# Attention beside a spectral filter on one core: the filter's last product with constants as weights in two parts, and output sums of eleven products for twelve

## The chip, the cores and the metric

The kernel runs on one core of a Trainium2 chip. The metric is the device time of one execution in microseconds, the median of the runs shown. The engines are TensorE (PE, with its weight loads listed as PEld), VectorE (DVE), ScalarE (ACT), GpSimd (POOL) and SyncE (SP); POOL, SP and ACT also issue DMAs, each in its own queue and in program order.

## The reference

Two independent computations of 2048 x 448 results, put side by side:

```python
# A: 16 heads of 28 columns, one shared key and value head
q = (x @ wq).reshape(B, S, H, Dh);  k = x @ wk;  v = x @ wv
p = softmax(einsum("bhqd,bkd->bhqk", q, k) * Dh ** -0.5)
a = einsum("bhqk,bkd->bhqd", p, v).reshape(B, S, H * Dh) @ wo
# B: a filter in the frequency domain
X = rfft2(x, axes=(-2, -1)) * (w_r + 1j * w_i)
b = irfft2(X, (S, D), axes=(-2, -1))
out = concatenate([a, b], axis=-1)
```

## The kernel before

**Precision by parts.** Most large products are made of reduced-precision float32 operands (F32R) in parts: an operand is cast to a high part, and the difference to the original is its low part. A product of two operands is then high x high + low x high + high x low.

**Attention.** The 16 heads stand as four groups g of four heads, each head in 32 rows, of which 28 are used; the four spare rows of the query weights carry columns for keys and values. Queries come in four chunks c of 512. A step is one key block of 128 for one (c, g): four score products (`score`, L1100), one for each head, each into one of seven PSUM banks; four exponentials on ACT (`exps`, L1117) from the bank into a p tile out of a ring of `P_BUFS`; and the value products (`values`, L1132) that read p and add up in bank 7. There are 256 steps. After 16 of them `group_out` (L986) copies bank 7 away, the sums of the exponentials go through DRAM and come back as a broadcast tile R by POOL's queue (L991 to L1000), and `group_norm` (L1008 to L1011) multiplies and splits the result into `oh` and `ol`. R's rows are all 32 of each head. When four groups of a chunk are done, four output units (`w_unit`, for 128 queries each) may run: `wo_mm` (L1020) makes 4 x 3 = 12 products of 448 columns, three for each group, and `wo_out` evicts. The last chunk's output products run at the very end (`partial`, and L1252 for its last group).

**Filter.** The first transform is done ahead of attention. While attention runs, DVE does a radix-2 transform in the tile X, multiplies by the filter and transforms back as background work (`forward`, `inverse`), and stores X to DRAM (`store`, L903). Then for each of eight q: `fft3_load` loads by POOL's queue, two `z_unit`s (L942) make products that DVE copies to SBUF (L948), and two `y_unit`s (L961) multiply by the cosine and sine constants cs3: each has four plain float32 products of 113 columns with z as the weights. DVE combines them (L966 to L975) and SP stores to ob (L977). The tiles of this stage are cut out of X's space (`carve`).

**The order.** It is written out by a plan in the kernel's own Python, which keeps a clock for PE, DVE and ACT with assumed durations, and emits the instructions of each engine in the order in which its loop (the `while done_steps < 256`) reaches them. A cycle of that loop is: scores, then the values of n steps. n is 4 if fill is at hand (over 1.0 us of it by the plan's durations), else 2. Fill are pieces of output units (0.605 each) and z and y units (0.88 each); output and filter units alternate where both are there. A piece is taken where at least six scores of the cycle have been made, two scores lie between pieces, and the cycle's quota (`share`, at least 1.6) isn't used up; the quota may be overrun by the last piece. The values of a cycle are emitted when their last exponential should be done and seven scores (`LEAD`) are ahead of them, or no bank is about to come free. A fill holds one of the seven banks until DVE has evicted it. DVE's work is an event list by the same clock (`after`) and a background list (`todo`).

Of the kernel before, what the change touches and what calls it, by code (L numbers as in the profile page):

```python
# [12 lines left out]
F32 = mybir.dt.float32  # L13
F32R = mybir.dt.float32r
# [3 lines left out]
ALU = mybir.AluOpType  # L18
# [4 lines left out]
S, D, H = 2048, 448, 16  # L23
DH = D // H
DF = D // 2 + 1
NG = 4
NC = 4
CW = 512
NK = 4
SCALE = DH ** -0.5  # L30
BOUND = float(np.float32(40.0 / SCALE))
P_BUFS = 20
LEAD = 7
WARM = 8, 8
FIRST = 8
# [60 lines left out]
def kernel(ctx: ExitStack, tc: tile.TileContext, t: dict):  # L96
    nc = tc.nc
    mm = nc.tensor.matmul

    cp = ctx.enter_context(tc.tile_pool(name="cp", bufs=1))  # L100
    dp = ctx.enter_context(tc.tile_pool(name="dp", bufs=1, space=DRAM))
# [6 lines left out]
    vs = cp.tile([128, 16, 32], F32, name="vs")  # L108
    cvec = cp.tile([128, NG, NC], F32, name="cvec")
    bits = cp.tile([1, 1], F32, name="bits")  # L110
    X = cp.tile([128, 2, 32, 113], F32, name="X")
    t1 = dp.tile([64, 2, 2, 32 * 113], F32, name="t1")
    t2 = dp.tile([128, 2, 32 * 113], F32, name="t2")

# [11 lines left out]
    fc, xb, ff = {}, {}, {}  # L126
# [86 lines left out]
    with tc.tile_pool(name="f1", bufs=2) as f1[0], tc.tile_pool(name="w1", bufs=1) as w1, ExitStack() as ctx1:  # L213
# [145 lines left out]

        def load_const(name, shape):  # L360
            def go():
                cons[name] = cp.tile(shape, F32, name=name)
                nc.sync.dma_start(cons[name], t[name])
            return add(SP, 0.4, go, loads[1, 1], kb=32)

# [294 lines left out]

    ap = ctx.enter_context(tc.tile_pool(name="ap", bufs=2))
    pp = ctx.enter_context(tc.tile_pool(name="pp", bufs=P_BUFS))
    V = nc.vector
    TT, STT = V.tensor_tensor, V.scalar_tensor_tensor

# [6 lines left out]
    def after(when, dur, f, *a):  # L672
        heapq.heappush(events, (when, next(serial), dur, f, a))
# [14 lines left out]
    def wide(n):  # L688
        return 0.165 + 0.00107 * n

    woh = ap.tile([128, NG, D], F32R, name="woh", bufs=1)
    wol = ap.tile([128, NG, D], F32R, name="wol", bufs=1)
    fc["cs3"] = ap.tile([113, 4, 113], F32, name="cs3", bufs=1)
    nc.gpsimd.dma_start(fc["cs3"], t["cs3"])

    late, held, early = {}, [None], deque()

# [62 lines left out]

    def wo_split(g):
        V.tensor_copy(woh[:, g], wo[g])
        TT(wol[:, g], wo[g], woh[:, g].bitcast(F32), op=ALU.subtract)


    t1v = t1.rearrange("(r k) l u (n f) -> r (k l u) n f", r=2, f=113)
# [139 lines left out]
                after(clk["dve"] + 3.0, 0.0, fft3_load, k)  # L906


    Xf = X.rearrange("p r n f -> p (r n f)")
    taken = [0]  # L910

    def carve(p, n):
        o = taken[0]
        taken[0] += n
        return Xf[:p, o:o + n]

    c2t = [carve(128, 904).rearrange("p (u j f) -> p u j f", u=2, f=113) for _ in range(2)]
    fit = [carve(128, 512).rearrange("p (j f) -> p j f", f=128) for _ in range(2)]
    zt = [[carve(113, 512).rearrange("p (r j n) -> p r j n", r=2, n=64) for _ in range(2)] for _ in range(2)]
    mt = [carve(128, 226).rearrange("p (k f) -> p k f", f=113) for _ in range(2)]  # L920
    y1t = [carve(128, 452).rearrange("p (k h f) -> p k h f", k=2, f=113) for _ in range(2)]
    yot = [carve(128, 452).rearrange("p (k f) -> p k f", f=113) for _ in range(2)]

    work = {"z": deque(), "w": deque()}
    cur, last_kind = [None], ["w"]
# [3 lines left out]
    def fft3_load(q):  # L929
        if q > 7:  # L930
            return
        nc.gpsimd.dma_start(c2t[q % 2].rearrange("p u j f -> p u (j f)"), t2[:, :, 452 * q:452 * q + 452])
        nc.gpsimd.dma_start(fit[q % 2], t["fi"][:, 4 * q:4 * q + 4])
        after(clk["dve"] + (10.0 if q < 2 else 6.0), 0.0, work["z"].extend, [z_unit(q, 0), z_unit(q, 1)])

    def z_unit(q, e):
        w = (113, 112)[e]

        def go(b):
            pz = view(bank[b], 4, 128)  # L940
            for j in range(4):
                mm(pz[:w, j], c2t[q % 2][:, e, j, :w], fit[q % 2][:, j], start=True, stop=True)  # L942
            if e == 1:
                after(clk["pe"] + 1.2, 0.0, fft3_load, q + 2)
            after(clk["pe"] + 1.2, 0.72, out, b)

        def out(b):
            V.tensor_copy(zt[q % 2][e][:w], view(bank[b], 4, 128)[:w].rearrange("p j (r n) -> p r j n", r=2))  # L948
            free[b] = clk["dve"] + 0.1
            if e == 1:  # L950
                after(clk["dve"] + 0.2, 0.0, work["z"].extendleft, [y_unit(q, 1), y_unit(q, 0)])
        return [(0.88, go)]

    def y_unit(q, v):
        js = slice(2 * v, 2 * v + 2)

        def go(b):
            py = view(bank[b], 4, 113)
            ze, zo = zt[q % 2]
            for k, (z, w, r) in enumerate(((ze, 113, 0), (zo, 112, 0), (zo, 112, 1), (ze, 113, 1))):  # L960
                mm(py[:, k], z[:w, r, js], fc["cs3"][:w, k], start=True, stop=True)  # L961
            after(clk["pe"] + 1.2, 1.2, out, b)

        def out(b):
            py, m, y1 = view(bank[b], 4, 113), mt[v], y1t[v]
            V.tensor_copy(m, py[:, 2:4])  # L966
            TT(y1[:, :, 0], py[:, 0:2], m, op=ALU.add)
            TT(y1[:, :, 1], py[:, 0:2], m, op=ALU.subtract)
            free[b] = clk["dve"] + 0.1
            after(clk["dve"], 0.8, last)  # L970

        def last():
            y1, yo = y1t[v], yot[v]
            TT(yo[:, 0:2], y1[:, 0], y1[:, 1], op=ALU.add)
            TT(yo[:, 2:4], y1[:, 0], y1[:, 1], op=ALU.subtract)  # L975
            r0 = (2 * q + v) * 128
            nc.sync.dma_start(t["ob"][r0:r0 + 128], yo)  # L977
        return [(0.88, go)]


    oh, ol, osb = {}, {}, {}
    normed, taken_out = [0] * NC, [0]

    def group_out(c, g):
# [10 lines left out]
    def group_sums(c, g, rs, rd):  # L995
        V.reciprocal(rs, rs)
        nc.gpsimd.dma_start(rd.rearrange("i (a b) -> (i a) b", b=16), rs)
        R = ap.tile([128, CW], F32, name="R", bufs=1)
        for i in range(4):
            nc.gpsimd.dma_start(R[32 * i:32 * i + 32], rd[i:i + 1].to_broadcast([32, CW]))  # L1000
        after(clk["dve"] + 12.0, 2.1, group_norm, c, g, R)

    def group_norm(c, g, R):
        if g == 0:
            oh[c] = ap.tile([128, NG, CW], F32R, name="oh")
            ol[c] = ap.tile([128, NG, CW], F32R, name="ol")
        o = osb[c, g]
        TT(o, o, R, op=ALU.mult)  # L1008
        h = oh[c][:, g]
        V.tensor_copy(h, o)  # L1010
        TT(ol[c][:, g], o, h.bitcast(F32), op=ALU.subtract)  # L1011
        normed[c] += 1
        if normed[c] == NG and c < NC - 1:
            after(clk["dve"] + 0.3, 0.0, work["w"].extend, [w_unit(c, k) for k in range(4)])

    def wo_mm(p, c, k, gs):
        s = slice(k * 128, k * 128 + 128)
        for g in gs:
            for n, (x, w) in enumerate(((oh, woh), (ol, woh), (oh, wol))):
                mm(p, x[c][:, g, s], w[:, g], start=(g == 0 and n == 0), stop=(g == NG - 1 and n == 2))  # L1020

    def wo_out(p, c, k):
        y = ap.tile([128, D], F32, name="ya")
# [17 lines left out]
    def w_unit(c, k):  # L1041
        def go(g):
            def f(b):
                wo_mm(bank[b][:, :D], c, k, (g,))
                if g == NG - 1:
                    after(clk["pe"] + 0.9, 0.65, out, b)
            return f

        def out(b):
            wo_out(bank[b][:, :D], c, k)  # L1050
            free[b] = clk["dve"] + 0.1
        return [(0.605, go(g)) for g in range(NG)]


    def switch(mode):
# [96 lines left out]
        for i in range(8):  # L1152
            after(18.0 + 2.0 * i, 0.0, spread, i)
    w0 = 5.0 if FIRST == 8 else 28.0
    for g in range(NG):
        after(w0 + 6 * g, 0.0, wo_load, g)
        after(w0 + 6.0 + 6 * g, 1.1, wo_split, g)
    for q in range(FIRST, 8):
        after(1.0 + 3.0 * (q - FIRST), 0.0, late_load, q)
        after(6.0 + 9.0 * (q - FIRST), 1.35, late_fold, q, 0)  # L1160
# [18 lines left out]
        b = 4 if rich else 2  # L1179
        return left if left < b + 2 else b  # L1180

    total = 12 * 4 * 0.605 + 32 * 0.88

    def share(n):
        return max(1.6, n * (total - done[0]) / max(250 - done_steps, 3)) if n > 2 else 0.0

    done_steps, quota = 0, 0.0
    n = size()
# [47 lines left out]
    c, g = NC - 1, NG - 1  # L1236
    o = osb[c, g] = qraw[:, g, c * CW:c * CW + CW]
    w3 = ap.tile([128, D], F32, name="w3", tag="ya")
    nc.sync.dma_start(w3, t["wo"][:, g])
# [69 lines left out]
def _layout(A_x, A_wq, A_wk, A_wv, A_wo, B_x, B_w_r, B_w_i):  # L1309
# [13 lines left out]
    z["wo"] = wo.reshape(NG, 128, D).transpose(1, 0, 2)  # L1323
# [18 lines left out]
def _gather(oa, ob):  # L1342
    out = np.empty((1, S, 2 * D), np.float32)
    out[0, :, :D] = oa
    y = ob.reshape(32, 64, 4, 113).transpose(1, 0, 2, 3).reshape(S, 4, 113)
    d = np.arange(113)
    b = out[0, :, D:]
    b[:, d] = y[:, 0]
    b[:, D - d[1:]] = y[:, 1, 1:]
    b[:, D // 2 - d[:112]] = y[:, 2, :112]  # L1350
    b[:, D // 2 + d[1:112]] = y[:, 3, 1:112]
    return out


_OUTS = {"oa": (S, D), "ob": (S, 4, 113)}


# [14 lines left out]
```

## Time and profile before

| | us |
|---|---|
| median of three runs (641.7 to 643.55) | 642.39 |
| the profiled execution | 641.98 |
| its span, first to last instruction | 640.1 |
| PE busy | 633.5 |
| ACT busy | 547.0 |
| DVE busy | 333.3 |

Attention's steps run from about 71 us to 626 us of the span. In the profile a line such as L1132 is a line of the kernel's file; "b L1132 x32" are the instructions that write a bank at that line. The value products show as eight records to a step, so x16 is two steps and x32 four.

### The profile page before, as it was taken

To read this page: it belongs to the slowest core of one execution; us is meant where nothing else is said; L and a number is where in the kernel's file an instruction comes from. 1 tells how busy PE (TensorE), PEld (TensorE's weight loads), DVE (VectorE), ACT (ScalarE), POOL (GpSimd) and SP (SyncE) were. 2 spreads that over 40 slices of the span, in tenths; PEclk is the share of its full clock that TensorE was granted. 3 is DMA by queue.
4 is the path that set the end of the run, shared out by engine and by line. 5 is a ranking of instruction groups with operands and counts; after the bars stand their busy time and mean duration, and the time that the engine had idled before them with its cause. 6 is when DMAs were issued, how large, how long until landed. Compare 5 with 4: busy or idle time off the path is not lost.

```text
span 640.1 us, 11636 instructions
## 1 busy us (share of the span) xinstructions
PE 633.5 (99%) x4380; PEld 358.5 (56%) x4380; DVE 333.3 (52%) x687; ACT 547.0 (85%) x1100; POOL 89.1 (14%) x164
## 2 busy tenths in 40 slices
PE   9999999999999999999999999999999999999997
PEld 7877544444444456554446655655665655564445
DVE  5999615979897977896323222215334310320014
ACT  4644899999999998889999879878888987888991
POOL 1021131101121101010122020020301101020200
PEclk9999999999999999999999999999999999999999
DMA  8766587030334121124444231132415131130002
GB/s 299 255 164 166 134 239 244 18 68 17 97 105 102 42 68 47 32 67 150 151 141 139 64 91 36 49 111 88 115 61 143 32 82 32 50 93 1 19 0 87
DMA packets 29667, 62.41 MB, mean 98 GB/s; under 512 B 6798, under 2 KB 18415, under 8 KB 28645
## 3 DMA queue, kind: packets, MB, share of 16 engines
q1 hardware_dynamic: 21850, 40.36, 23.1%
q0 software_dynamic: 7328, 20.72, 10.8%
q8 instruction: 35, 0.57, 0.4%
q10 hardware_dynamic: 432, 0.57, 0.3%
q14 instruction: 22, 0.18, 0.1%
HBM read 29.63 MB, written 15.02 MB: 70 GB/s over the span
## 4 chain that ended last, share of the span: by engine, by line
PE 88%; ACT 0%; issue 0%; DVE 0%; ACTq 0%
PE b L1100 41%; PE b L1132 36%; PE b L1020 6%; PE b L961 2%; PE b L942 2%; PE b L1252 0%; PE b L163 0%; ACT yb L1035 0%; DVE yb L1038 0%; ACTq L1036 0%
## 5 line engine op out<-in xcount | busy, mean ns | idle before, releaser
L1117 ACT ACTIVATE p<-b 128x512 f32<-128x512 f32 x1024 | 506.7, 768 | 46.4 <-PE b L1100 45.4
L1100 PE MATMUL b<-qa,ka 128*128 128x512 f32 x1024 | 284.7, 411 | 0.5 <-PEq L617 0.5
L1100 PEld LDWEIGHTS b<-qa,ka 128*128 128x128 f32 x1024 | 182.1, 188 | 128.2 <-ACT p L1117 83.9
L1132 PE MATMUL b<-p,vs 128*32 128x512 f32 x2048 | 240.0, 597 | 0.0
L1132 PEld LDWEIGHTS b<-p,vs 128*32 128x32 f32 x2048 | 56.5, 109 | 120.9 <-issue 119.3
L986 DVE COPY qraw<-b 128x512 f32<-128x512 f32 x15 | 10.4, 692 | 82.0 <-PE b L1132 82.0
L1024 DVE COPY ya<-b 128x448 f32<-128x448 f32 x12 | 7.5, 624 | 65.1 <-PE b L1020 64.0
L991 POOL DMA_DIRECT2D sd<-qraw x15 | 8.8, 587 | 218.8 <-DVE qraw L986 218.8
L827 DVE SCALAR_TENSOR_TENSOR X<-w,X 128x226 f32<-128x226 f32 (+2 forms) x72 | 34.1, 473 | 2.4
L1000 POOL DMA_DIRECT2D R<-rd x60 | 30.2, 508 | 34.9 <-DMA rd<-rs 34.9
L966 DVE COPY X<-b 128x226 f32<-128x226 f32 x16 | 6.2, 390 | 45.3 <-ACT p L1117 43.9
L321 ACT ACTIVATE qraw<-b 128x512 f32<-128x512 f32 x16 | 9.4, 599 | 19.5 <-PE b L317 19.4
L948 DVE COPY X<-b 113x512 f32<-113x512 f32 (+1 forms) x16 | 11.1, 691 | 28.6 <-ACT p L1117 22.7
L317 PE MATMUL b<-xh,wqh 128*128 128x512 f32 x64 | 24.6, 416 | 0.4 <-DVE xh L265 0.4
L1008 DVE TENSOR_TENSOR qraw<-qraw,R 128x512 f32<-128x512 f32 x15 | 10.3, 685 | 26.7 <-DMA R<-rd 26.7
L317 PE MATMUL b<-xh,wql 128*128 128x512 f32 x64 | 23.0, 390 | 0.0
L1020 PE MATMUL b<-woh,oh 128*128 128x448 f32 x60 | 22.1, 369 | 0.0
L1020 PE MATMUL b<-wol,oh 128*128 128x448 f32 x60 | 22.0, 366 | 0.0
L1020 PE MATMUL b<-woh,ol 128*128 128x448 f32 x60 | 21.9, 366 | 0.0
L820 DVE SCALAR_TENSOR_TENSOR w<-X 128x113 f32<-128x113 f32 (+2 forms) x56 | 17.7, 353 | 0.1
L961 PEld LDWEIGHTS b<-cs,X 113*128 113x128 f32 (+1 forms) x128 | 16.8, 191 | 1.4
L317 PE MATMUL b<-xl,wqh 128*128 128x512 f32 x48 | 17.3, 391 | 0.0
(113 smaller groups left out, 511.4 us busy)
## 6 DMA issues: line engine op xcount, KB each, us to landing
qa<-qa SPq DMA_DIRECT2D x15, 512.0 KB
X<-t POOLq DMA_DIRECT2D x16, 452.0 KB, 5.4
xb<-xb SPq DMA_DIRECT2D x8, 512.0 KB
qa<-qh SPq DMA_DIRECT2D x60, 64.0 KB
qa<-ql SPq DMA_DIRECT2D x60, 64.0 KB
R<-rd POOLq DMA_DIRECT2D x60, 64.0 KB, 2.2
t<-bs SPq DMA_DIRECT2D x16, 226.0 KB
wf<-w POOLq DMA_DIRECT2D x8, 452.0 KB, 4.2
```

Of the source, the lines that this page charges most:

```text
L317: mm(pq[c, g], w[:, j, gs], x[:, j], start=(j == 0 and n == 0), stop=(j == 3 and n == 1))
L820: STT(out, y, sy, x, op0=ALU.mult, op1=ALU.add if c > 0 else ALU.subtract)
L827: todo(226 * n, lambda d=d, q=q: STT(both(d), t[0].rearrange("p r n f -> p r (n f)"), q, both(a), op0=ALU.mult, op1=ALU.add))
L942: mm(pz[:w, j], c2t[q % 2][:, e, j, :w], fit[q % 2][:, j], start=True, stop=True)
L948: V.tensor_copy(zt[q % 2][e][:w], view(bank[b], 4, 128)[:w].rearrange("p j (r n) -> p r j n", r=2))
L961: mm(py[:, k], z[:w, r, js], fc["cs3"][:w, k], start=True, stop=True)
L986: V.tensor_copy(o, bank[7])
L1000: nc.gpsimd.dma_start(R[32 * i:32 * i + 32], rd[i:i + 1].to_broadcast([32, CW]))
L1020: mm(p, x[c][:, g, s], w[:, g], start=(g == 0 and n == 0), stop=(g == NG - 1 and n == 2))
L1100: mm(bank[b], ka[:, kc * 128:(kc + 1) * 128], qa[c, g][:, h], start=True, stop=True)
L1117: nc.scalar.activation(p, bank[b], AF.Exp, scale=SCALE)
L1132: mm(bank[7][32 * i:32 * i + 32], vs[:, kc], pt.pop(4 * st + i), start=(kc == 0), stop=(kc == 15))
```

## The change

In the filter's last product the constants become the weights, in a high and a low part (`csh`, `csl`), and z the moving operand, also split into two parts by DVE at its eviction. A y unit is then two sums of three F32R products of 256 columns in place of four plain float32 products of 113. The result stands transposed, and ob's layout changes with it; DVE's last two operations are done once for a pair of units.

In the output product of the first three chunks, the low part of group 0's result is stored to DRAM (`lows`) and loaded from there into the spare rows of `oh` (four groups) and of `ol` (groups 1 to 3). The output weights carry group 0's rows in their spare rows, in seven variants. So the product of group 0's low part needs no instruction of its own: 11 products for 12. R is filled in 28 of 32 rows only, its spare rows are set to zero once. The output units become available 7.0 us after the last norm by the plan's clock (0.3 before).

For the space of this, `P_BUFS` goes from 20 to 17, X moves to a pool of its own that is closed when the last filter stage opens (`fft3_open`), and some constants move to a pool of the start. cs3's load moves from the start of attention to `fft3_open`. The plan's durations and the quota's least value change.

```diff
-P_BUFS = 20
+P_BUFS = 17
...
-    X = cp.tile([128, 2, 32, 113], F32, name="X")
...
     pp = ctx.enter_context(tc.tile_pool(name="pp", bufs=P_BUFS))
+    xp = ctx.enter_context(ExitStack())
+    X = xp.enter_context(tc.tile_pool(name="xp", bufs=1)).tile([128, 2, 32, 113], F32, name="X")
...
-    woh = ap.tile([128, NG, D], F32R, name="woh", bufs=1)
+    woh = ap.tile([128, 7, D], F32R, name="woh", bufs=1)
     wol = ap.tile([128, NG, D], F32R, name="wol", bufs=1)
-    fc["cs3"] = ap.tile([113, 4, 113], F32, name="cs3", bufs=1)
-    nc.gpsimd.dma_start(fc["cs3"], t["cs3"])
+    csh = ap.tile([113, 4, 113], F32R, name="csh", bufs=1)
+    csl = ap.tile([113, 4, 113], F32R, name="csl", bufs=1)
...
     def wo_split(g):
         V.tensor_copy(woh[:, g], wo[g])
-        TT(wol[:, g], wo[g], woh[:, g].bitcast(F32), op=ALU.subtract)
+        if g < NG:
+            TT(wol[:, g], wo[g], woh[:, g].bitcast(F32), op=ALU.subtract)
...
+    def fft3_open():
+        xp.close()
+        p3 = xp.enter_context(tc.tile_pool(name="p3", bufs=2))
+        for q in range(2):
+            fb["c2", q] = p3.tile([128, 2, 4, 113], F32, name="c2")
+            fb["fi", q] = p3.tile([128, 4, 128], F32, name="fi")
+            for e in range(2):
+                fb["z", q, e] = [p3.tile([113, 2, 4, 64], F32R, name=f"z{n}{e}") for n in "hl"]
+        cs = scratch()[:113, :452].rearrange("p (k f) -> p k f", k=4)
+        nc.gpsimd.dma_start(cs, t["cs3"])
+        todo(452, lambda: V.tensor_copy(csh, cs))
+        todo(452, lambda: TT(csl, cs, csh.bitcast(F32), op=ALU.subtract))
...
     def z_unit(q, e):
...
-            after(clk["pe"] + 1.2, 0.72, out, b)
+            after(clk["pe"] + 1.2, 1.4, out, b)
 
         def out(b):
-            V.tensor_copy(zt[q % 2][e][:w], view(bank[b], 4, 128)[:w].rearrange("p j (r n) -> p r j n", r=2))
+            pz = view(bank[b], 4, 128)[:w].rearrange("p j (r n) -> p r j n", r=2)
+            h, l = (x[:w] for x in fb["z", q % 2, e])
+            V.tensor_copy(h, pz)
+            TT(l, pz, h.bitcast(F32), op=ALU.subtract)
...
     def y_unit(q, v):
-        js = slice(2 * v, 2 * v + 2)
 
         def go(b):
-            py = view(bank[b], 4, 113)
-            ze, zo = zt[q % 2]
-            for k, (z, w, r) in enumerate(((ze, 113, 0), (zo, 112, 0), (zo, 112, 1), (ze, 113, 1))):
-                mm(py[:, k], z[:w, r, js], fc["cs3"][:w, k], start=True, stop=True)
-            after(clk["pe"] + 1.2, 1.2, out, b)
+            py = view(bank[b], 2, 256)
+            for k in range(2):
+                kind, e, r = ((0, 0, 0), (2, 1, 1), (1, 1, 0), (3, 0, 1))[2 * v + k]
+                w = (113, 112)[e]
+                zh, zl = (x[:w, r].rearrange("p j n -> p (j n)") for x in fb["z", q % 2, e])
+                for n, (c, z) in enumerate(((csh, zh), (csh, zl), (csl, zh))):
+                    mm(py[:113, k], c[:w, kind], z, start=(n == 0), stop=(n == 2))
+            after(clk["pe"] + 1.2, 2.65 if v else 1.25, out, b)
 
         def out(b):
...
+            y = y1[v] = scratch()[:113, :768].rearrange("p (s n) -> p s n", s=3)
+            V.tensor_copy(y[:, 2], py[:, 1])
+            TT(y[:, 0], py[:, 0], y[:, 2], op=ALU.add)
+            TT(y[:, 1], py[:, 0], y[:, 2], op=ALU.subtract)
+            free[b] = clk["dve"] + (-1.3 if v else 0.1)
+            if v:
+                a, c = y1.pop(0), y1.pop(1)
+                for h, op in enumerate((ALU.add, ALU.subtract)):
+                    last(h, op, a, c)
+
+        def last(h, op, a, c):
+            yo = fp.tile([113, 2, 256], F32, name="yo", tag="bs")
+            TT(yo, a[:, :2], c[:, :2], op=op)
+            nc.sync.dma_start(t["ob"][:, q, h], yo)
+        return [(0.73, go)]
...
+    R = ap.tile([128, CW], F32, name="R", bufs=1)
+    V.memset(R, 0.0)
...
         for i in range(4):
-            nc.gpsimd.dma_start(R[32 * i:32 * i + 32], rd[i:i + 1].to_broadcast([32, CW]))
+            nc.gpsimd.dma_start(R[32 * i:32 * i + DH], rd[i:i + 1].to_broadcast([DH, CW]))
...
-        if normed[c] == NG and c < NC - 1:
-            after(clk["dve"] + 0.3, 0.0, work["w"].extend, [w_unit(c, k) for k in range(4)])
+        if c < NC - 1:
+            if g == 0:
+                lows[c] = dp.tile([128, CW], F32, name="lows", bufs=2)
+                nc.sync.dma_start(lows[c], ol[c][:, 0].bitcast(F32))
+            rows = lows[c].rearrange("(i m r) n -> r i m n", i=4, r=4)
+            if g == NG - 1:
+                for r in range(4):
+                    nc.sync.dma_start(oh[c][DH + r::32].bitcast(F32), rows[r, :, :4])
+                    nc.sync.dma_start(ol[c][DH + r::32, 1:].bitcast(F32), rows[r, :, 4:7])
+                after(clk["dve"] + 7.0, 0.0, work["w"].extend, [w_unit(c, k) for k in range(4)])
...
-            for n, (x, w) in enumerate(((oh, woh), (ol, woh), (oh, wol))):
-                mm(p, x[c][:, g, s], w[:, g], start=(g == 0 and n == 0), stop=(g == NG - 1 and n == 2))
+            spare = c < NC - 1
+            for n, (x, w, m) in enumerate(((oh, woh, g), (oh, wol, g), (ol, woh, g + 3 * spare))):
+                if n < 2 or g or not spare:
+                    mm(p, x[c][:, g, s], w[:, m], start=(g == 0 and n == 0), stop=(g == NG - 1 and n == 2))
...
-        return [(0.605, go(g)) for g in range(NG)]
+        return [(0.605 if g else 0.403, go(g)) for g in range(NG)]
...
-    for g in range(NG):
-        after(w0 + 6 * g, 0.0, wo_load, g)
-        after(w0 + 6.0 + 6 * g, 1.1, wo_split, g)
+    for g in range(7):
+        at = w0 + 6 * g if g < NG else 60.0 + 6 * g
+        after(at, 0.0, wo_load, g)
+        after(at + 6.0, 1.1, wo_split, g)
...
-    total = 12 * 4 * 0.605 + 32 * 0.88
+    total = 12 * 2.22 + 16 * (0.88 + 0.73)
 
     def share(n):
-        return max(1.6, n * (total - done[0]) / max(250 - done_steps, 3)) if n > 2 else 0.0
+        return max(1.8, n * (total - done[0]) / max(250 - done_steps, 3)) if n > 2 else 0.0
...
+    wo = wo.reshape(NG, 4, 32, D)[[0, 1, 2, 3, 1, 2, 3, 3]]
+    wo[:7, :, DH:] = wo[0, :, :DH].reshape(4, 7, 4, D).transpose(1, 0, 2, 3)
+    z["wo"] = wo.reshape(8, 128, D).transpose(1, 0, 2)
...
-_OUTS = {"oa": (S, D), "ob": (S, 4, 113)}
+_OUTS = {"oa": (S, D), "ob": (113, 8, 2, 2, 256)}
```

More of the change, by code (lines that the diff above doesn't have):

```diff
@@ L361, in go @@
             def go():
-                cons[name] = cp.tile(shape, F32, name=name)
+                cons[name] = (cp if name in ("mask", "ident") else w1).tile(shape, F32, name=name)
                 nc.sync.dma_start(cons[name], t[name])
@@ L906, in store @@
                 after(clk["dve"] + 3.0, 0.0, fft3_load, k)
[L909 to L922, printed above, removed]
+    fb = {}
+    def fft3_open():
[10 more added lines that the diff above has]
+        todo(452, lambda: TT(csl, cs, csh.bitcast(F32), op=ALU.subtract))
     work = {"z": deque(), "w": deque()}
@@ L931, in fft3_load @@
             return
-        nc.gpsimd.dma_start(c2t[q % 2].rearrange("p u j f -> p u (j f)"), t2[:, :, 452 * q:452 * q + 452])
-        nc.gpsimd.dma_start(fit[q % 2], t["fi"][:, 4 * q:4 * q + 4])
+        if not fb:
+            fft3_open()
+        nc.gpsimd.dma_start(fb["c2", q % 2].rearrange("p u j f -> p u (j f)"), t2[:, :, 452 * q:452 * q + 452])
+        nc.gpsimd.dma_start(fb["fi", q % 2], t["fi"][:, 4 * q:4 * q + 4])
         after(clk["dve"] + (10.0 if q < 2 else 6.0), 0.0, work["z"].extend, [z_unit(q, 0), z_unit(q, 1)])
@@ L941, in go @@
             for j in range(4):
-                mm(pz[:w, j], c2t[q % 2][:, e, j, :w], fit[q % 2][:, j], start=True, stop=True)
+                mm(pz[:w, j], fb["c2", q % 2][:, e, j, :w], fb["fi", q % 2][:, j], start=True, stop=True)
             if e == 1:
                 after(clk["pe"] + 1.2, 0.0, fft3_load, q + 2)
-            after(clk["pe"] + 1.2, 0.72, out, b)
+            after(clk["pe"] + 1.2, 1.4, out, b)
         def out(b):
-            V.tensor_copy(zt[q % 2][e][:w], view(bank[b], 4, 128)[:w].rearrange("p j (r n) -> p r j n", r=2))
+            pz = view(bank[b], 4, 128)[:w].rearrange("p j (r n) -> p r j n", r=2)
+            h, l = (x[:w] for x in fb["z", q % 2, e])
+            V.tensor_copy(h, pz)
+            TT(l, pz, h.bitcast(F32), op=ALU.subtract)
             free[b] = clk["dve"] + 0.1
@@ L952, in z_unit @@
         return [(0.88, go)]
+    y1 = {}
     def y_unit(q, v):
-        js = slice(2 * v, 2 * v + 2)
         def go(b):
-            py = view(bank[b], 4, 113)
-            ze, zo = zt[q % 2]
-            for k, (z, w, r) in enumerate(((ze, 113, 0), (zo, 112, 0), (zo, 112, 1), (ze, 113, 1))):
-                mm(py[:, k], z[:w, r, js], fc["cs3"][:w, k], start=True, stop=True)
-            after(clk["pe"] + 1.2, 1.2, out, b)
-        def out(b):
[L965 to L981, printed above, removed]
+            py = view(bank[b], 2, 256)
[5 more added lines that the diff above has]
+                    mm(py[:113, k], c[:w, kind], z, start=(n == 0), stop=(n == 2))
@@ new lines, in go @@
+            after(clk["pe"] + 1.2, 2.65 if v else 1.25, out, b)
+        def out(b):
+            py = view(bank[b], 2, 256)[:113]
+            y = y1[v] = scratch()[:113, :768].rearrange("p (s n) -> p s n", s=3)
[7 more added lines that the diff above has]
+                    last(h, op, a, c)
@@ L982 @@
+        def last(h, op, a, c):
[3 more added lines that the diff above has]
+        return [(0.73, go)]
+    oh, ol, osb, lows = {}, {}, {}, {}
+    R = ap.tile([128, CW], F32, name="R", bufs=1)
+    V.memset(R, 0.0)
     normed, taken_out = [0] * NC, [0]
@@ L997, in group_sums, with group_norm @@
         nc.gpsimd.dma_start(rd.rearrange("i (a b) -> (i a) b", b=16), rs)
-        R = ap.tile([128, CW], F32, name="R", bufs=1)
         for i in range(4):
-            nc.gpsimd.dma_start(R[32 * i:32 * i + 32], rd[i:i + 1].to_broadcast([32, CW]))
-        after(clk["dve"] + 12.0, 2.1, group_norm, c, g, R)
-    def group_norm(c, g, R):
+            nc.gpsimd.dma_start(R[32 * i:32 * i + DH], rd[i:i + 1].to_broadcast([DH, CW]))
+        after(clk["dve"] + 12.0, 2.1, group_norm, c, g)
+    def group_norm(c, g):
         if g == 0:
@@ L1238 @@
     w3 = ap.tile([128, D], F32, name="w3", tag="ya")
-    nc.sync.dma_start(w3, t["wo"][:, g])
+    nc.sync.dma_start(w3, t["wo"][:, 7])
     for k in range(4):
@@ L1322, in _layout @@
     wo[:, :DH] = np.asarray(A_wo).reshape(H, DH, D)
-    z["wo"] = wo.reshape(NG, 128, D).transpose(1, 0, 2)
+    wo = wo.reshape(NG, 4, 32, D)[[0, 1, 2, 3, 1, 2, 3, 3]]
+    wo[:7, :, DH:] = wo[0, :, :DH].reshape(4, 7, 4, D).transpose(1, 0, 2, 3)
+    z["wo"] = wo.reshape(8, 128, D).transpose(1, 0, 2)
     bt = np.asarray(B_x)[0].reshape(64, 32, D).transpose(2, 1, 0)[:, _points()].reshape(D, S)
@@ L1344, in _gather @@
     out[0, :, :D] = oa
-    y = ob.reshape(32, 64, 4, 113).transpose(1, 0, 2, 3).reshape(S, 4, 113)
+    y = ob.reshape(113, 8, 4, 4, 64).transpose(4, 1, 3, 2, 0).reshape(S, 4, 113)
     d = np.arange(113)
```

## The prediction

> **What bounds the kernel now.** I read the page's head, then the chain that ended last, then the timeline of single cycles, then the groups by line.
>
> ```profile
> span 640.1 us, 11636 instructions
> PE 633.5 (99%) x4380; PEld 358.5 (56%) x4380; DVE 333.3 (52%) x687; ACT 547.0 (85%) x1100; POOL 89.1 (14%) x164
> ```
>
> At 99% PE looks like the bound, and one would take off every matmul that the change removes. But matmul ends are modelled, so a PE that waits between two matmuls can still show as busy. The chain shows the waiting. Attention is a sequence of cycles: scores (L1100), perhaps some other products as fill, then the value products (L1132) of 2 or 4 key steps. Columns: start, duration, piece. First a stretch without fill, 11 cycles of 2 steps from the first to the last row:
>
> ```profile
> 578.71 2.11 PE b L1100 x8
> 580.82 1.85 PE b L1132 x16
> ...
> 622.23 0.66 PE b L1100 x2
> ```
>
> 43.52 us for 22 steps are 1.978 us a step, 7.91 for four. Now a 4-step cycle with three pieces of the output product, and a run of cycles with filter work:
>
> ```profile
> 240.71 1.59 PE b L1100 x6
> 242.30 0.60 PE b L1020 x3
> 242.90 0.45 PE b L1100 x2
> ...
> 245.05 1.69 PE b L1100 x6
> 246.73 3.57 PE b L1132 x32
> 250.30 1.59 PE b L1100 x6
> ```
> ```profile
> 344.40 1.59 PE b L1100 x6
> 346.00 0.88 PE b L961 x8
> ...
> 349.94 3.57 PE b L1132 x32
> 353.51 1.59 PE b L1100 x6
> ...
> 363.10 1.60 PE b L1100 x6
> ```
>
> The first lasts 9.59 us (240.71 to 250.30), the next 9.11 (to 353.51), the next 9.59. These lengths stand 0.48 apart, and why shows in the timeline (start, duration, engine, line; in brackets the idle time before and its releaser):
>
> ```profile
> 341.91 1.57 ACT L1117 ACTIVATE p<-b 128x512 f32<-128x512 f32 x3 [0.18 <-PE b L1132]
> 344.33 1.66 PE L1100 MATMUL b<-qa,ka 128*128 128x512 f32 x6
> 344.87 7.46 ACT L1117 ACTIVATE p<-b 128x512 f32<-128x512 f32 x15 [1.39 <-PE b L1100]
> 349.44 0.19 PEld L1100 LDWEIGHTS b<-qa,ka 128*128 128x128 f32 x1 [0.22 <-ACT p L1117]
> 349.87 3.64 PE L1132 MATMUL b<-p,vs 128*32 128x512 f32 x32
> 353.98 8.44 ACT L1117 ACTIVATE p<-b 128x512 f32<-128x512 f32 x17 [1.65 <-PE b L1100]
> ```
>
> An exponential takes 7.46 / 15 = 0.497 us. During the values ACT lives on scores computed ahead, at most as many as there are free banks of 7. Then it idles (1.39, 1.65 us) until the first new score, which PE reaches 3.57 after the values began (349.94 to 353.51); its exponential comes 0.54 after the score (344.33 to 344.87). So a 4-step cycle is: values 3.57, score to exponential 0.54, (16 - lead) exponentials, and 0.5 from the last needed one to the values. With lead 7 that is 3.57 + 0.54 + 9 x 0.497 + 0.5 = 9.1, with 6 it is 9.6, with 5 10.1. The lead is 7 less the banks which a fill still holds. This is the bound: cycles with fill cost a nearly fixed surcharge over 7.91, set by banks and by ACT, and PE work lies just beneath it. PE alone in the 9.59 cycle: 3.57 + 1.59 + 3 x 0.61 + 2 x 0.45 + 6 x 0.23 = 9.27.
>
> All cycles with fill lie in three stretches: 231.16 to 278.86, 334.30 to 513.73, 521.78 to 578.71.
>
> ```profile
> 231.16 1.58 PE b L1100 x6
> ...
> 278.86 2.11 PE b L1100 x8
> ```
> ```profile
> 513.73 2.31 PE b L1100 x9
> ...
> 521.78 1.58 PE b L1100 x6
> ```
>
> In them I counted 5, 19 and 6 cycles: 47.70 + 179.43 + 56.93 = 284.06 us for 120 steps, which at 1.978 would take 237.4. The surcharge of all fill is 46.7 us in 30 cycles, 1.56 each. That is what the change can alter; elsewhere it adds little.
>
> **The change part by part.** *Output product of eleven.* Twelve output units (three query chunks, four each) lose one of twelve products of about 0.203 us (0.60 / 3): 12 x 0.203 = 2.4 us of PE. The first piece falls to 0.40. The quota of fill per cycle goes from 1.6 to 1.8: three pieces (0.403 + 0.605 + 0.605 = 1.61 by the kernel's own durations) don't use it up, so the fourth goes in too, and a unit takes one cycle where it took 1.33. That cycle on PE: 3.57 + 1.59 + 0.40 + 3 x 0.61 + 3 x 0.46 + 4 x 0.23 = 9.69, just over the ladder's 9.6; surcharge 1.78.
>
> *Filter's last product.* A y unit was 0.88 for 8 records (two to a plain f32 product); 16 units. It becomes 6 f32r products of 256 columns. f32r products of 448 and 512 columns are spaced 0.203 and about 0.23, so 0.42 ns a column, and 256 columns come to 0.122: 0.73 a unit, 2.4 us less in all. Bounds: 0.65 a unit at the z products' spacing (0.87 / 8, below); upward, if a weight load doesn't hide under so short a product, load and product one after the other, 6 x (0.19 + 0.12) = 1.86. I take 0.73, since here loads of 0.19 already run at a spacing of 0.11:
>
> ```profile
> L961 PEld LDWEIGHTS b<-cs,X 113*128 113x128 f32 (+1 forms) x128 | 16.8, 191 | 1.4
> L948 DVE COPY X<-b 113x512 f32<-113x512 f32 (+1 forms) x16 | 11.1, 691 | 28.6 <-ACT p L1117 22.7 <-PE b L942 5.9
> L966 DVE COPY X<-b 128x226 f32<-128x226 f32 x16 | 6.2, 390 | 45.3 <-ACT p L1117 43.9 <-PE b L961 1.4
> L974 DVE TENSOR_TENSOR X<-X 128x226 f32<-128x226 f32 x16 | 6.3, 394 | 0.5
> ```
>
> A rule speaks against that row: the Trainium skill, "TensorE: Matmul & The Clock Gate", section "The mechanism", says that weight loads overlap running matmuls only where the row group differs. By it each y unit would pay load and product in turn; the trace disagrees, with 191 ns loads spaced 110.
>
> *DVE.* Eviction of z was one copy, 0.69; now copy and subtraction, 1.38, and 16 x 0.69 = 11 us more. y was five operations of 0.39, 1.95 a unit; now three of 256 columns (0.42 between the rows of 226 and 512) and, per pair of units, two of 512 (0.69): 1.95 a unit again. DVE is 52% busy and less than that late, so its time is hidden; its latency isn't: a z unit holds its bank 0.69 longer, which lowers the lead.
>
> *Three fills in a cycle.* z, z (2 x 0.87 = 1.74, or 1.76 by the kernel's durations) no longer exhaust 1.8, so filter cycles take three units. The trace has a cycle with a like fill, 0.62 + 2 x 0.87 = 2.36:
>
> ```profile
> 334.30 1.60 PE b L1100 x6
> 335.90 0.62 PE b L1020 x3
> ...
> 336.98 0.87 PE b L942 x8
> ...
> 339.19 1.65 PE b L1100 x7
> 340.83 3.57 PE b L1132 x32
> ```
>
> It lasts 10.10 (334.30 to 344.40) with 17 scores. After the change z, z, y is 2.47 and y, y, z 2.33: on PE 9.95 and 9.81 with 16 scores. Between 9.8 (PE only) and 10.6 (two banks held, 10.1, and one more exponential's wait for a bank) I take 10.0, nearest to the row with this fill: surcharge 2.09.
>
> *Seventeen p tiles for twenty.* A lead exponential beyond the first now waits until the first value step has released its tile; with twenty this hit the fifth, which started at 341.91, 1.15 after those values began. So with 17 six exponentials run from 1.15 to 1.15 + 6 x 0.497 = 4.13, and the first new score reaches ACT at 3.57 + 0.54 = 4.11. ACT's idle time moves from the end of the values to their start; cost 0.02 a cycle, 0.5 us at most in all, and up to 1.49 (three exponentials) a cycle if that cover fails. Without fill the run needs 8 + 7 = 15 tiles: no cost.
>
> *DMAs and queues.* Per chunk one store of the low part and eight loads of spare rows are put on SP, behind DVE's last norm; the plan holds the output units back 7 us for them. Prices:
>
> ```profile
> 365.29 0.59 SPq L207 DMA_DIRECT2D qa<-ql  x1
> ```
> ```profile
> R<-rd POOLq DMA_DIRECT2D x60, 64.0 KB, 2.2
> X<-fi POOLq DMA_DIRECT2D x8, 256.0 KB, 4.0
> ```
> ```profile
> 222.56 0.69 DVE L1011 TENSOR_TENSOR ol<-qraw,oh 128x512 fp32r<-128x512 f32 x1
> ...
> 232.58 0.37 PE L1020 MATMUL b<-woh,oh 128*128 128x448 f32 x1
> ```
>
> Eight issues of 0.59 and a landing of about 2.2 end 6.9 after the norm. Output products now start 9.3 after it (223.25 to 232.58); the plan's 6.7 more keeps them clear. Behind these issues on SP wait the q loads of a group that is due 30 us later, and the stores of ob: hidden; uncovered, 4.7 us a chunk. The ob stores stay 16 of 226 KB. On POOL the filter constants' load moves from the start to just ahead of the first z loads, and DVE waits some 4 us for it; the first z product is planned 10 us after, so it costs nothing unless a group's eviction falls just there (then up to 4). Three more wo loads, three casts of about 0.4, a memset and two operations for the constants lie on DVE in the fill-free early part.
>
> *Sum.* Output chunks one and three: 8 cycles x 1.78 = 14.2. Chunk two shares cycles with the filter (one unit of 0.8 to two or three pieces): 6 x 1.69 = 10.1 at 9.6 each. The other 28 filter units, three a cycle: 9.33 x 2.09 = 19.5. Together 43.8 against 46.7: 2.9 us off, in 23 cycles for 30. The profiled execution took 641.98, its span 640.1; 639.1 from there, and its distance to the median of 642.39 (0.41) makes it 639.2 to 639.5. I say 639.2.
>
> **Rivals.**
> *All PE savings arrive.* If triple cycles run at PE's 9.8 and the others at 9.6, the surcharge is 14 x 1.69 + 9.33 x 1.9 = 41.4: 5.3 off, 636.7 to 637.1. For it: PE is the upper term in triples. Against: banks.
> *Units merely packed tighter.* Before, two filter units cost a mean of 1.44 (9.11 and 9.59), 0.72 a unit. At 10.2 a triple costs 2.29, 0.76 a unit. The filter then loses 32 x 0.04 = 1.3 and eats half of what the output units bring: 641 to 642, no change. For it: the 10.10 row.
> *Starved ACT (slower).* The place is ACT's wait for p tiles at the start of the values; it decides as soon as the six lead exponentials end later than 4.11 after that start. Should release come 0.5 later, or the values be held by an exponential that twenty tiles let run ahead, 23 cycles x 0.5 = 11.6 us: 650.7. For it: the margin is 0.02. Against: ACT idles 1.39 to 1.65 a cycle now. A milder form, triples at 10.6, costs 9.33 x 0.6 = 5.6 and gives 645.
> *Weight loads not hidden (slower).* 16 x (1.86 - 0.88) = 15.7 us more on PE, and that is past every slack: 655. Against: the 191 ns row.
>
> **How the numbers follow.** Forecast 0.48, all savings 0.07, packed tighter 0.20, starved ACT in either form 0.20, loads not hidden 0.05. A measurement can tell about 0.3%, 1.9 us, so 640.5 to 644.3 is no change. Faster 0.55, the first two; same 0.20; slower 0.25. The range runs from 635.5, a little under all savings, to 646, over the milder form of starving; what lies outside is the rest of the slower cases. For faster alone it is 636 to 640.5.
>
> **What would show it.** In the chain: about 23 pieces of 32 value products where 30 stood; output cycles with four pieces at about 9.7; triples near 10.0; a y unit of 0.73 for six records. On ACT: the idle time ahead of the first new score nearly gone, and about 1.1 at the start of the values, released by L1132. Wrong would be: triples at 10.5 or more, cycles without fill over 7.95 for four steps, output products waiting for DMAs, or as many cycles with fill as before.

## The result, and the profile after

The changed kernel takes 684.94 us (median; 682.69 to 687.28), the kernel before 642.06 beside it: 1.0664 times as long, interval 1.0636 to 1.0691. Forecast were 639.2 us and a chance of 0.25 for slower, and the range ended at 646. The forecast was wrong by 45 us and in its sign, and no rival of it named the cause.

The head of the page after, and from its fourth part the chain that ended last, by line:

```profile
span 684.5 us, 11647 instructions
PE 639.1 (93%) x4336; PEld 357.0 (52%) x4336; DVE 347.9 (51%) x693; ACT 548.1 (80%) x1100; POOL 91.3 (13%) x167
...
PE   9999799999999999999997699999636999999997
...
PEclk9999899999999999999999799999858999999999
...
PE b L1124 32%; PE b L1156 29%; DMA ob<-yo 16%; PE b L316 6%; PE b L1044 5%; PE b L152 2%; ACT p L1141 1%; PE b L162 1%; PE b L946 1%; PE b L241 1%; DVE yo L989 0%; DMA ka<-kl 0%; PE b L1277 0%; PE b L972 0%; DMA ol<-lows 0%
```

PE has holes now (slices 22, 23 and 29 to 31; slice 5 is the start of attention), and a DMA that no line of before's chain knew holds 16% of the span: the store of the filter's result. Who waits for it stands in the list of waits (waiter and line, what it waited for: us in total, times, longest):

```profile
DVE yo L989 <- DMA ob<-yo: 48.6, 7, 9.9
PEld b L1124 <- DVE zl L955: 33.9, 4, 16.2
PE b L1124 <- DVE zl L955: 21.3, 2, 15.3
PE b L1124 <- DMA ol<-lows: 10.1, 1, 10.1
PE b L1124 <- DVE w L980: 3.1, 1, 3.1
```

PE's four long pauses in the filter's stretch, the last three rows, come to 34.5 us. `zl` and `w` are evictions by DVE.

The first such chain in the timeline (start, duration, engine or queue, line; idle time before and its releaser in brackets):

```profile
357.16 1.29 DVE L989 TENSOR_TENSOR yo<-w 113x512 f32<-113x512 f32 x2
357.88 4.93 SPq L990 DMA_DIRECT2D ob<-yo  x2
362.86 8.85 SPq L1034 DMA_DIRECT2D oh<-lows  x1
371.43 0.69 DVE L989 TENSOR_TENSOR yo<-w 113x512 f32<-113x512 f32 x1 [4.51 <-DMA ob<-yo]
371.84 0.49 PE L1124 MATMUL b<-qa,ka 128*128 128x512 f32 x1
380.40 0.69 DVE L989 TENSOR_TENSOR yo<-w 113x512 f32<-113x512 f32 x1 [8.27 <-DMA ob<-yo]
381.73 0.69 DVE L955 TENSOR_TENSOR zl<-b,zh 113x512 fp32r<-113x512 f32 x1
382.47 2.63 PEld L1124 LDWEIGHTS b<-qa,ka 128*128 128x128 f32 x7 [10.45 <-DVE zl L955]
382.47 3.30 PE L1124 MATMUL b<-qa,ka 128*128 128x512 f32 x7 [10.14 <-DMA ol<-lows]
```

Two stores of 226 KB are issued at 357.9. The first of two yo tiles is free again at 371.4, the second at 380.4, 9.0 us later. DVE works in order: the eviction at 381.73, which gives PE a bank, comes only after its two waits for yo. PE makes nothing from 372.3 to 382.5; its weight load waits for that eviction, and the product itself is put down to the last load of the low part, which stood on SP behind the same stores. Before, no store to ob appeared among the waits. The next view gives busy time in a stretch, then the granted clock, the share of the 16 DMA engines and GB/s:

```profile
366.00:371.00 5.00, 5.00 (x43) 2.66 (x45) 0.89 (x3) 3.19 (x8) 0.00 (x0) 1.00 0.07 26
376.00:380.00 4.00, 0.00 (x0) 0.00 (x0) 0.00 (x0) 0.00 (x0) 0.00 (x0) 0.50 0.08 30
```

And the kernel before in the middle of one of its stores:

```profile
350.50:352.00 1.50, 1.50 (x18) 0.39 (x12) 0.08 (x1) 1.50 (x4) 0.00 (x0) 1.00 0.37 140
```

One engine of 16 is a share of 0.0625. The store of 113 rows moves 26 GB/s on 0.07, that of 128 rows 140 GB/s on 0.37. At 26 GB/s 226 KB (231,424 bytes) take 8.9 us, close to the 9.0 that lie between the two releases. At that rate the sixteen stores need 16 x 9.0 = 144 us of that one engine, in the stretch where the filter's work is crowded.

The second loss is at the start of attention:

```profile
77.63 0.48 DVE L996 MEMSET R<- 128x512 f32 x1 [4.33 <-DMA ka<-kl]
78.03 1.09 DVE L178 COPY bs<-b 128x452 f32<-128x452 f32 x2
79.18 3.64 PE L1156 MATMUL b<-p,vs 128*32 128x512 f32 x16 [3.11 <-DVE bs L178]
```

The new memset of R waits for the DMAs that read `kl`, the keys' low part. That tile's pool is closed before R's is opened, so R can lie in the same place, as the wait suggests. The eviction of a filter bank stands behind the memset, and the first values behind that. They begin 2.9 us later than before (76.31 in the same view), and take 3.64 us where 1.92 is usual, at a lower clock behind the pause:

```profile
80.00:82.00 2.00, 2.00 (x16) 0.39 (x8) 1.44 (x4) 0.00 (x0) 0.00 (x0) 0.50 0.82 237
```

### The profile page after: what moved, and what is told of

The parts are those of the page before. It is cut to its first block, busy times and chain, and to the rows that moved or that the text cites. A ratio compares the mean times of both kernels' runs of the same rounds, so it can differ in the third digit from the quotient of the medians.

```text
span 684.5 us, 11647 instructions
## 1 busy us (share of the span) xinstructions
PE 639.1 (93%) x4336; PEld 357.0 (52%) x4336; DVE 347.9 (51%) x693; ACT 548.1 (80%) x1100; POOL 91.3 (13%) x167
## 4 chain that ended last, share of the span: by engine, by line
PE 77%; DMA 17%; DVE 2%; ACT 2%; issue 1%; SPq 0%; POOL 0%; ACTq 0%; DVEq 0%; POOLq 0%
PE b L1124 32%; PE b L1156 29%; DMA ob<-yo 16%; PE b L316 6%; PE b L1044 5%; PE b L152 2%; ACT p L1141 1%; PE b L162 1%; PE b L946 1%; PE b L241 1%; DVE yo L989 0%; DMA ka<-kl 0%; PE b L1277 0%; PE b L972 0%; DMA ol<-lows 0%
## 5 line engine op out<-in xcount | busy, mean ns | idle before, releaser
L1124 PE MATMUL b<-qa,ka 128*128 128x512 f32 x1024 | 289.1, 415 | 35.1 <-DVE zl L955 21.3
L1124 PEld LDWEIGHTS b<-qa,ka 128*128 128x128 f32 x1024 | 185.3, 192 | 164.4 <-ACT p L1141 82.2
L1156 PE MATMUL b<-p,vs 128*32 128x512 f32 x2048 | 244.9, 604 | 3.1 <-DVE bs L178 3.1
L989 DVE TENSOR_TENSOR yo<-w 113x512 f32<-113x512 f32 x16 | 10.8, 691 | 48.8 <-DMA ob<-yo 48.6
L978 DVE COPY w<-b 113x256 f32<-113x256 f32 x16 | 6.8, 424 | 36.2 <-PE b L972 34.9
L946 PE MATMUL b<-fi,c 128*112 128x128 f32 (+1 forms) x128 | 16.7, 273 | 1.5 <-DVE zl L955 1.5
L946 PEld LDWEIGHTS b<-fi,c 128*112 128x112 f32 (+1 forms) x128 | 16.1, 177 | 3.5 <-DVE zl L955 1.9
L1044 PE MATMUL b<-woh,ol 128*128 128x448 f32 x48 | 17.6, 366 | 0.0
```

The source lines that it names most:

```text
L946: mm(pz[:w, j], fb["c2", q % 2][:, e, j, :w], fb["fi", q % 2][:, j], start=True, stop=True)
L989: TT(yo, a[:, :2], c[:, :2], op=op)
L1044: mm(p, x[c][:, g, s], w[:, m], start=(g == 0 and n == 0), stop=(g == NG - 1 and n == 2))
L1124: mm(bank[b], ka[:, kc * 128:(kc + 1) * 128], qa[c, g][:, h], start=True, stop=True)
L1156: mm(bank[7][32 * i:32 * i + 32], vs[:, kc], pt.pop(4 * st + i), start=(kc == 0), stop=(kc == 15))
```

## The experiments

Theory S: a store of 113 rows issued by SP runs through one DMA engine, and two yo buffers carry its 9 us to DVE and PE. Rivals: D, the rows of 2 KB lie 32 KB apart in DRAM; L, the low part's loads on SP stall PE. Theory M: the memset's place costs the start. Beneath these, theory C is the forecast's own ledger (cycles with fill pay a surcharge set by banks and ACT), against E (PE time counts).

**Stores split.**

```diff
-            nc.sync.dma_start(t["ob"][:, q, h], yo)
+            nc.sync.dma_start(t["ob"][:112, q, h], yo[:112])
+            nc.sync.dma_start(t["ob"][112:, q, h], yo[112:])
```

> The changed kernel with each store to ob made as two, of 112 rows and of one row. Theory S (a store of 113 rows, issued by SP, goes through a single DMA engine, about 9.4 us for 226 KB, and two buffers of yo pass that wait on to DVE and from there to PE): DVE's wait for ob disappears from the list of waits, and the time falls to 645 to 648 us, which is the forecast of 639.2 and 5.7 lost at the start of attention. Theory D (the store is slow because its 2 KB rows lie 32 KB apart in DRAM): unchanged at 683 to 687. Theory L (the low part's way through DRAM on SP's queue is what stalls): above 675.

640.1 us, 0.9935 of the kernel before (0.9909 to 0.9960). One row taken off each store gives back 7.3% (1.0664 less 0.9935). DVE's wait for ob is gone from the list, and SP issues at once:

```profile
364.15 1.29 DVE L989 TENSOR_TENSOR yo<-w 113x512 f32<-113x512 f32 x2
364.87 0.33 SPq L990 DMA_DIRECT2D ob<-yo  x1
365.24 0.28 SPq L991 DMA_DIRECT2D ob<-yo  x1
```

L falls: its loads are all still there. The time is 5 us under the lower end of what I expected: the start costs less than I took, and the rest gains a little more.

**The same store to one contiguous stretch.**

```diff
-            nc.sync.dma_start(t["ob"][:, q, h], yo)
+            nc.sync.dma_start(t["ob"][q, h], yo)
...
-_OUTS = {"oa": (S, D), "ob": (113, 8, 2, 2, 256)}
+_OUTS = {"oa": (S, D), "ob": (8, 2, 113, 2, 256)}
```

> The changed kernel with ob laid out so that each store of 113 rows goes to one contiguous stretch of DRAM. S: unchanged, 683 to 687 us, with DVE still waiting about 49 us for ob. D: 645 to 648. L: unchanged as well.

683.92 us, 1.0629 (1.0586 to 1.0671): nothing gained, and in the middle of a store

```profile
362.00:368.00 6.00, 6.00 (x49) 3.47 (x51) 1.79 (x5) 4.18 (x10) 0.00 (x0) 1.00 0.07 26
```

D falls.

**The same store from POOL.**

```diff
-            nc.sync.dma_start(t["ob"][:, q, h], yo)
+            nc.gpsimd.dma_start(t["ob"][:, q, h], yo)
```

> The changed kernel with the same stores of 113 rows issued from POOL in place of SP. S, if the single engine belongs to SP's way of dividing a store: POOL's loads of 113 rows landed in 3.6 to 5.1 us, so the stores land in under 6 and the time is 645 to 652, POOL's other work delaying some. S, if it belongs to the shape whatever the queue: 683 or more. D: 683 or more. L: 683 or more, or somewhat less since the loads of the low part stand no longer behind the stores on SP.

639.46 us, 0.9931 (0.9908 to 0.9955), 5.5 us under the 645 to 652 that I expected. The stores land in 3.3 us (median; 2.6 to 5.3). The same 113 rows issued by POOL cost nothing that can be measured beside the split ones. So it is neither the shape nor the queue alone, but the two together: 113 rows in a DMA of SP. Other awkward counts were not tried.

**The cause put into the kernel before.**

```diff
-            nc.sync.dma_start(t["ob"][r0:r0 + 128], yo)
+            nc.sync.dma_start(t["ob"][r0:r0 + 113], yo[:113])
+            nc.sync.dma_start(t["ob"][r0 + 113:r0 + 128], yo[113:])
```

> The kernel before with each of its 16 stores of 128 rows made as two on SP, of 113 rows and of 15; everything else as it was. S: the larger store runs at one engine's rate, some 12 to 13 packets of 1.8 KB a us, 8.6 to 9 us for 204 KB, 17 to 18 us for a pair, about as long as the kernel before takes between two pairs (18.7); so the profile shows long store times, SP held at their issue, and the time rises only a little, 0 to 10 us. If the slowness came from the changed kernel's layout or from its other loads (D, L): stores as quick as before, and the time unchanged within 2 us.

650.88 us, 1.0102 (1.0062 to 1.0142), with SP held at the issue of the second pair:

```profile
353.07 0.93 SPq L977 DMA_DIRECT2D ob<-X  x1
354.05 8.09 SPq L978 DMA_DIRECT2D ob<-X  x1
```

Only the cut of the rows differs from before, and 6.7 us come with it. The doubled number of stores is not the reason: the split of 112 and 1 doubles it too. The loss is smaller than in the changed kernel, as expected, since here the filter's pairs come little faster than the one engine drains them. They do come faster at times: DVE waits for ob six times, 26.6 us in all, where the changed kernel has seven waits and 48.6 us.

**The memset later.** On top of the split stores:

```diff
     R = ap.tile([128, CW], F32, name="R", bufs=1)
-    V.memset(R, 0.0)
...
+    after(14.0, 0.5, lambda: V.memset(R, 0.0))
```

> The changed kernel with split stores, and with the memset of R some 14 us later in the plan. Theory M (the memset waited 4.3 us on DVE for the loads of the keys' low part, whose tile R's space overlaps, and the first filter eviction and the first values stood behind it): 5 to 6 us below the kernel with split stores alone, 639 to 642. Rival: the late start is made up for later by cycles with more ready work, no more than 2 us below it.

637.77 us, 0.9914 (0.9877 to 0.9950). The first values begin at 77.07 in place of 78.93 with split stores alone, and the spans are 634.9 and 636.9. M's place is shown by the trace. Its size is some 2 us and not 5 to 6: in the profiled execution with split stores alone PE stands 1.27 us for the memset's sake, where the changed kernel's trace has 3.11. The code up to there is the same in both; the pause was shorter because PE came later to that place. The 5.7 which I had read off the changed kernel's start (third values at 90.15 for 84.46) held, besides the wait, the slower clock after it. The two times alone, with overlapping intervals, would not show M, and starts vary: POOL's stores with the late memset (below) begin their first values at 80.39 in the profiled execution.

**The parts alone.** The filter's part, with split stores, 17 p tiles, quota 1.8, and the old output product (the diff cut to its core):

```diff
-P_BUFS = 20
+P_BUFS = 17
...
+                for n, (c, z) in enumerate(((csh, zh), (csh, zl), (csl, zh))):
+                    mm(py[:113, k], c[:w, kind], z, start=(n == 0), stop=(n == 2))
...
-    total = 12 * 4 * 0.605 + 32 * 0.88
+    total = 12 * 4 * 0.605 + 16 * (0.88 + 0.73)
```

> The filter's part alone: constants as weights in two parts, split stores, 17 p tiles, quota 1.8, with the output product of twelve as before. Theory C (cycles with fill pay a surcharge set by banks and ACT; it falls with their number): the filter's units in threes cost 32/3 x 2.0 = 21 us for 23 before, the output pieces stay three to a cycle: 1 to 3 us below the kernel before. Rival E (what counts is PE time): 16 units shorter by 0.17, 2.7 us below. Both parts together measured 5.9 below.

642.51 us, 0.9984 (0.9956 to 1.0011): no change that can be told. The output part, with the old filter:

```diff
-P_BUFS = 20
+P_BUFS = 17
...
+            for n, (x, w, m) in enumerate(((oh, woh, g), (oh, wol, g), (ol, woh, g + 3 * spare))):
+                if n < 2 or g or not spare:
+                    mm(p, x[c][:, g, s], w[:, m], start=(g == 0 and n == 0), stop=(g == NG - 1 and n == 2))
...
-    total = 12 * 4 * 0.605 + 32 * 0.88
+    total = 12 * 2.22 + 32 * 0.88
-        return max(1.6, n * (total - done[0]) / max(250 - done_steps, 3)) if n > 2 else 0.0
+        return max(1.75, n * (total - done[0]) / max(250 - done_steps, 3)) if n > 2 else 0.0
```

> The output part alone: sums of eleven, low part by DRAM, R cleared late, 17 p tiles, the filter as before and its stores of 128 rows; quota 1.75, so that a unit's four pieces go into one cycle and filter units stay in pairs. C: 12 cycles of surcharge 1.8 for 16 of about 1.5 to 1.7, 2.4 to 4 us below the kernel before. E: 2.4 us below. Rival Q (the loads on SP delay the queries' loads): at or above the kernel before.

639.87 us, 0.9947 (0.9924 to 0.9971), 3.4 us below. Each part takes some 2.5 us off PE by the forecast's count; one shows and one doesn't. That fits C better than E, but the first interval reaches to 0.9956, 2.8 below, so it doesn't exclude E. Nor do the chains bear C out in full. The filter's part has 27 cycles with fill, 260.7 us for 108 steps, a surcharge of 47.1 where the kernel before has 46.7: three cycles fewer, each longer. The output part has 28, 266.7 us for 112 steps, a surcharge of 45.2; the larger share of its gain, 2.4 us, lies in the steps without fill (1.951 us each for 1.968), for which C has no term. The output part's time excludes Q, by which it would not be below the kernel before.

**Seventeen p tiles in the kernel before.**

```diff
-P_BUFS = 20
+P_BUFS = 17
```

> The kernel before with 17 p tiles for 20 and nothing else. Forecast: no change, 0.5 us at most, ACT's idle time of 1.4 to 1.7 us a cycle moving from the end of the values to their start. Rival, starved ACT: 0.5 a cycle with fill, 15 us in 30 cycles, 657.

643.72 us, 1.0004 (0.9978 to 1.0030): no cost. The timeline shows the idle time moved, as forecast, to just after the values began:

```profile
428.85 3.64 PE L1132 MATMUL b<-p,vs 128*32 128x512 f32 x32
429.99 7.97 ACT L1117 ACTIVATE p<-b 128x512 f32<-128x512 f32 x16 [1.64 <-PE b L1132]
...
437.94 3.64 PE L1132 MATMUL b<-p,vs 128*32 128x512 f32 x32
439.09 2.56 ACT L1117 ACTIVATE p<-b 128x512 f32<-128x512 f32 x5 [1.13 <-PE b L1132]
```

ACT starts again 1.14 and 1.15 after the values began; 1.15 was the forecast's number.

**The quota smaller.** Split stores and late memset as above, and:

```diff
-        return max(1.8, n * (total - done[0]) / max(250 - done_steps, 3)) if n > 2 else 0.0
+        return max(1.45, n * (total - done[0]) / max(250 - done_steps, 3)) if n > 2 else 0.0
```

> The changed kernel with split stores and late memset, its quota of fill 1.45 in place of 1.8: two filter units or three output pieces to a cycle, the same PE work. C: 28 to 30 cycles with fill at about 9.5 in place of 23 at about 9.75, surcharge 46 to 48 in place of 43: 3 to 6 us above the kernel with quota 1.8 (637.8), 641 to 644. E: unchanged within 1 us, since the PE work is the same.

642.45 us, 0.9979 (0.9961 to 0.9997), against 0.9914: with the same PE work 0.65% above the quota of 1.8, and the two intervals don't meet. By the chain it has 31 cycles of four steps, 292.1 us for 124 steps, a surcharge of 46.8, where the quota of 1.8 has 23 and 43.0. E can't give that; C was asked for 641 to 644 and a surcharge of 46 to 48. This is the run that decides against E.

**POOL's stores and the late memset**, the best version found:

> The changed kernel with the late memset and its whole stores of 113 rows issued from POOL. S, with the single engine belonging to SP's way of dividing a store: 637 to 639 us, 0.8% below the kernel before, the same as with split stores and late memset. If POOL's descriptors cost its other work time: up to 641.

637.89 us, 0.9900 (0.9870 to 0.9929), not told apart from split stores with the late memset.

## Why the prediction was wrong

**The step that failed** is under DMAs and queues: "The ob stores stay 16 of 226 KB." They were priced by bytes and count, that is at nothing, though the change turned their source from 128 rows to 113. Each took about 9.0 us of one engine. The diff showed the shape, and the profile of before even has loads of 113 rows at 3.6 us (cs3), but by POOL. The Trainium skill states what was overlooked ("DMA: Bandwidth & Descriptors", section "Why a DMA increments its semaphore by 16 and not by 1"): a DMA of SP uses the largest number of engines, at most 16, that divides the slowest dimension of both its sides, here the rows, so a prime 113 leaves one, while some copies issued from POOL are spread all the same. The trace agrees: a share of 0.07, and 112 + 1 rows or POOL give the time back.

**The second step** was "a memset and two operations for the constants lie on DVE in the fill-free early part", again at nothing. It cost 1.27 us of PE in the trace with split stores, and 1.6 to 2.3 by two pairs of medians with overlapping intervals, through a tile's place and an in-order queue.

**What stood.** With both losses removed the ledger's totals came out close to its own numbers, in part by luck. Rows of the kernel with split stores and late memset, from the chain: a cycle with a whole output unit, and a cycle of y, y, z:

```profile
259.43 1.60 PE b L1124 x6
...
264.65 0.92 PE b L1124 x4
265.57 3.57 PE b L1156 x32
269.14 1.59 PE b L1124 x6
```
```profile
347.49 1.60 PE b L1124 x6
349.09 0.72 PE b L972 x6
350.27 0.71 PE b L972 x6
351.46 0.87 PE b L946 x8
352.33 1.40 PE b L1124 x6
353.73 3.57 PE b L1156 x32
357.30 1.59 PE b L1124 x6
```

- Output cycle 9.71 us (259.43 to 269.14), forecast 9.69. This cycle 9.81 (347.49 to 357.30); eight cycles with three filter units average 9.90, forecast 10.0.
- A y unit takes 0.72, forecast 0.73. Its six weight loads, 0.18 us each, stand 0.12 apart, so they hide under products of 256 columns: the rival "not hidden" falls.
- Cycles with fill: 23, forecast 23. Their sum is 224.9 us for 92 steps; less 92 x 1.978 the surcharge is 43.0, forecast 43.8 for 46.7 before. That the totals agree so well is partly luck: eight cycles of three filter units stand where 9.33 were forecast, and the third chunk, forecast as four cycles of whole units, has five of 9.16 to 10.09 with three filter units among them.
- Seventeen tiles cost nothing: "starved ACT" falls.
- DVE waited 10.1 us for the filter's constants, forecast some 4; the chain shows nothing held up by it.
- The gain, 0.86% or 5.5 us (3.2 to 7.9), is more than the 2.9 forecast. In the profiled executions the chain from the first values to the last is 6.2 us shorter: 3.7 of it is the surcharge, the rest lies in the steps without fill, 1.954 us each for 1.968. Their cycles of two steps come in two lengths, 3.92 and 3.96 us; the forecast's 1.978 a step is the longer one. The kernel before has 25 of the longer, also with 17 p tiles, this kernel 11, the output part alone none. What causes the longer kind stays open.

Most of the gain came with the output part, in its cycles and in the steps without fill; the filter part, whose matmuls really became shorter, gave by itself nothing that can be told. The ledger had it at 21 us for 23, and its chain shows no such fall.

## What to carry to other kernels

When a change turns a tile's orientation, price its DMAs again by the number of rows and the issuing queue, not by bytes: cut an awkward count into one that divides well and a rest, or issue it elsewhere. A new instruction without work still has a place in memory and in a queue; ask whose tile lay there and who stands behind it. And where a cycle's length is set by buffers, count the cycles, and what each of them costs, before counting matmuls.

## What the runs showed of the hardware

PE's four pauses come to 34.5 of the 44.8 us that split stores give back. The rest was not taken apart, but PE's granted clock fell to half during and after the pauses, and work at half speed takes longer. The view of spans and clocks of the changed kernel:

```profile
core 0: 684.5 us, clock 0.968
```

If the only states are full and half speed, a mean of 0.968 over 684.5 us is 44 us at half speed (0.032 x 684.5 / 0.5). The stretch 376 to 380 above, with PE idle, stands at 0.50. After the last such stall

```profile
527.00 1.65 PE b L1124 x3
528.64 3.57 PE b L1156 x16
532.22 2.14 PE b L1124 x8
534.35 1.85 PE b L1156 x16
```

two steps of values take 3.57 us and the next two 1.85, and the granted clock of the two stretches is 0.50 and 1.00:

```profile
528.64:532.21 3.57, 3.57 (x18) 0.60 (x17) 0.00 (x0) 0.82 (x2) 0.00 (x0) 0.50 0.08 30
534.35:536.20 1.85, 1.85 (x18) 0.41 (x17) 0.00 (x0) 1.85 (x5) 0.00 (x0) 1.00 0.46 125
```

With the stores split the mean was 0.997. The Trainium skill says the same ("TensorE: Matmul & The Clock Gate", "What's actually happening"): the clock goes to half after an idle window of some 3.4 us. No run here measures that window; a PE pause of 3.11 us at the start was followed by slow values, one of 1.27 was not. Nor do the traces show a pause as the only way to it: with split stores the clock is 0.50 from 72 to 74 us, where PE shows busy throughout, and behind a stretch, 60 to 70 us, at 1.00 in which PE was busy for 9.36 of 10 us.
